# Visits of step pairs, of one output group around an attention product, or of two quarter output steps, with sums moved

## The chip, the cores and the metric

The kernel runs on one core of a Trainium2 chip. Its engines are TensorE (PE, the matmuls; PEld is its loading of weights), VectorE (DVE), ScalarE (ACT), GpSimd (POOL) and SyncE (SP, which issues transfers). SBUF is the on-chip memory that all engines read; PSUM is the small accumulator memory that PE writes, here 8 banks of 128 x 512 f32. The metric is the device time of one execution in microseconds (us).

## The reference

Attention of 8 batches, 12 heads, 448 positions and head dimension 64; its output, with the heads laid side by side, is the input of a gated feed-forward layer.

```python
scores = np.matmul(q, k.transpose(0, 1, 3, 2)) / np.sqrt(64)      # 8 x 12 x 448 x 448
attn = softmax(scores)                                             # over the last axis
x = np.matmul(attn, v).transpose(0, 2, 1, 3).reshape(3584, 768)
g, val = x @ w_gate, x @ w_val                                     # 768 -> 1536
out = (g * sigmoid(g) * val) @ w_out                               # 1536 -> 768, 3584 x 768 f32
```

## The kernel before

**The plan of visits.** Two heads make a pair, so there are 48 pairs, six to a batch. Two batches make a block of 896 tokens, held turned as `X[kk]` (768 features as 6 column blocks of 128 rows); there are four blocks. A loop (`for x, (chunks, todo) in enumerate(plan)`) walks some 50 visits. A visit issues up to three score chunks (a chunk is 128 keys of both heads against 448 queries, matmuls into the score tile `s`, L327 and L357, then one exponential on ACT, L347 or L365, into `E`), the product of one earlier pair with its values (`pv`, matmuls into two accumulators `acc`, L418), and feed-forward work. A visit without a product is called bare.

**Tiles in PSUM.** Score tiles come from the pool `ps_s`: three of two banks each. Single banks come from `ps_f`, which has two. `ps_s` also serves the gates, the output groups and the units below; `ps_f` serves the accumulators, the values and the plain outputs. A tile that is asked for waits until the last reader of the one it replaces has finished.

**A product.** `pv_open` takes the two accumulators, `pv_rest` multiplies the remaining 64 keys (8 matmuls), `pv_quad` the three full chunks (24 matmuls), and `pv_close` divides on DVE by the row sum (reciprocal L443, multiply L444). `turn_x` then transposes the result into `X` by a transfer on SP's queue (L485, L489). `copy_v` (L218, DVE) turns a pair's values into the form that the product reads; `load_v` and `load_keys` fetch them through POOL's queue (L177).

**A step** is one of 12 slices of 128 hidden units for 384 or 512 tokens: six gate matmuls (`gp`, L548), the tanh on ACT (`sg`, L573), six value matmuls (L548), and on DVE `(sg + 1) * gp` (L596) and the close, which writes `hts` (L601). `run_fv` runs one step, `run_pair` two at once with both gates ahead of the values. `run_single` runs one alone and sets `split`: the value product is then done in two halves of the tokens, the first into the second bank of the gate's score tile. A step with `late` leaves the last column block's matmuls to the end.

**An output group** (`out_group`) multiplies 256 tokens by 384 output columns as a 2 x 2 block with seven products instead of eight. Its inputs are sums: `h_sums` (L531 to L534, on `hts`) and `out_sums` (L523 to L526, on the output weights), all on DVE and all with both inputs in SBUF. Its first half is three products of six matmuls into the banks `a`, `c` and `b` of one score tile (L664). Then `p1` is kept from `a` (on ACT at L705, or with `own` on DVE at L703), `p15` from `c` (L706), and `c` is corrected from `b` (L708), for the second half adds to `c`:

```python
product(a, hh(0, x), bb(0, 0), True)
product(c, hh(0, y), tt(0))
...
apart(product(b, hs(0), tt(1), True), keep1, keep15)
nc.vector.scalar_tensor_tensor(c, p15[:], HS, b, ALU.mult, ALU.add)
yield
product(b, hs(1), tt(2))
```

The second half is products into `b`, `a`, `c` and `b`, with `part` (L712) and the last row (L718) on DVE and the first row on ACT (L683), into `osb`, which is stored.

**What sets the order.** Every engine runs its own instructions in the order in which they are emitted, so the order is that of the code. Up to visit 18 a budget (`run_budget`) deals out steps and outputs; from `base` = 19 the table `VISITS` does, one entry for each visit: the block that begins, the number of steps, of output groups, of quarter output steps (`plain_out`, 12 matmuls of 128 x 192 at L635), and of sums taken from the list `sums`:

```python
begins, nf, ng, no, ns = VISITS[x - base]
...
add_sum(ns)
if ng == 1:
    run_group(nf, gate_first=bare)
```

Here `run_group` puts a step into a group; in most visits of the table the product comes first, then a group with one step inside it, or a single step.

**After the visits**, from about 321 us, come the half block (512 tokens of `X[3]`) and then the last block of 448-wide units. In these parts `Unit` computes a gate or value product as a 2 x 2 block with seven products: P1 to P7 (PE, L778), a zero product Z (L815), A1 and A2 (ACT, L820, L824), two corrections D1 and D2 (DVE, L827, L831) that later products add to, and outputs (`out`, L843 on ACT, L845 on DVE). P1 reads the block's tokens as they are; the others need four token sums (`token_sums`, L973 to L976) and four weight sums for each unit (`weight_sums`, L741 to L744 on POOL, both inputs in SBUF). The two parts' order is worked out by `order_of`, a planner with a cost for each item; POOL's weight sums `W_5` to `W_11`, the first group's h sums `H0` to `H3` and a plain output `O` are items of it. Ahead of it stand P1 and P5 of units 0 and 1 and then the last pair's product. Behind the half block's units come its four output groups (`run_groups(groups5)`, L664), which take one sum from `sums` after each half, then the last units and the last output groups.

**Where sums lie.** `wsum_space` and `token_space` cut buffers that are free by then into the places of these sums. The half block's four token sums are emitted one to a visit in visits 47 to 50, weight sums of units 0 to 3 in visit 46 and of unit 4 after the loop. The last units' token sums (128 x 1344 each, into a buffer of the pool that holds `X`) wait in `sums` behind the second group pair's h sums and run on DVE during the half block's groups.

## Time and profile before

| | |
|---|---|
| Median of 3 runs (lowest, highest) | 449.44 us (449.36, 449.75) |
| Profiled execution | 449.9 us, of which the span is 448.1 |
| Granted TensorE clock | 1.00 |
| PE busy | 425.7 us (95%), 4594 matmuls |
| DVE, ACT, POOL busy | 268.2, 246.8, 226.3 us |
| Transfers | 50.01 MB, 112 GB/s mean |

The trace gives the following starts, in us from the start of the span:

| Place | Start |
|---|---|
| visit 13 (budget) | 91.6 |
| visit 19 (first of the table) | 125.6 |
| visit 35 | 224.3 |
| visit 46 | 289.5 |
| visit 50 | 310.2 |
| half block's units | 321.5 |
| half block's output groups | 355.7 |
| last units | 370.6 |
| end of the last output groups | 444 |

How to read the lines. In the busy table each engine has its busy time, its share of the span and its instructions (the number after x). The slices cut the span into 40 equal parts; a digit is the busy share in tenths, and 9 is 90% or more. A timeline line gives the start, the busy time, the engine, the line of the code, the operation, what it writes and from what, the tile's size, its type and a count when several instructions are drawn together; in square brackets stands how long the engine had been idle just before, with the engine, tile and line that ended the wait. An idle engine that is not the bottleneck costs nothing.

### The profile page before, as it was taken

How to read it: one execution, taken by the hardware profiler on the slowest of the kernel's cores; microseconds unless marked ns; L12 is line 12 of the kernel's file. 1: busy time of each engine (PE TensorE's matmuls, PEld its weight loads, DVE VectorE, ACT ScalarE, POOL GpSimd, SP SyncE). 2: the span in 40 equal slices, each digit the busy share in tenths (PEclk: the TensorE clock that was granted, in tenths of full speed). 3: DMA queues.
4: the chain of work that ended last, by engine and by line, in shares of the span. 5: the costliest groups of instructions: out<-in, count | busy, mean ns of one | idle time of the engine just before them, and what ended most of it. 6: DMA issues, size and time to landing. Idle time of an engine off the chain costs nothing.

```text
span 448.1 us, 11507 instructions
## 1 busy us (share of the span) xinstructions
PE 425.7 (95%) x4594; PEld 285.9 (64%) x4594; DVE 268.2 (60%) x643; ACT 246.8 (55%) x393; POOL 226.3 (51%) x349
## 2 busy tenths in 40 slices
PE   8999999999999999998999799998999899999996
PEld 3666565554647767565655576765888795555695
DVE  4666562865667655664544755556567665575663
ACT  6976677555555665745565555557365325545321
POOL 8755724999885647377357838601797000000000
PEclk9999999999999999999999999999999999999999
DMA  9999999999999999899899976313300022000124
GB/s 138 185 199 201 198 170 162 135 199 187 155 141 120 137 119 135 141 128 144 138 101 121 168 99 133 65 23 92 88 24 1 13 79 70 1 0 0 37 72 142
DMA packets 108742, 50.01 MB, mean 112 GB/s; under 512 B 60896, under 2 KB 105568, under 8 KB 108688
## 3 DMA queue, kind: packets, MB, share of 16 engines
q0 software_dynamic: 46912, 24.75, 48.3%
q1 hardware_dynamic: 61632, 24.34, 31.1%
q8 instruction: 36, 0.59, 0.5%
q14 instruction: 18, 0.15, 0.2%
q10 hardware_dynamic: 144, 0.17, 0.1%
HBM read 49.55 MB, written 11.01 MB: 135 GB/s over the span
## 4 chain that ended last, share of the span: by engine, by line
PE 77%; DVE 9%; ACT 7%; DMA 3%; issue 2%; POOL 1%; SPq 0%; DVEq 0%; POOLq 0%; ACTq 0%
PE og L664 16%; PE gp L548 14%; PE vp L548 10%; PE un L778 9%; PE ub L778 7%; PE acc L418 7%; ACT E L347 4%; PE s L327 3%; DVE hts L601 2%; PE s L357 2%; PE op L635 2%; PE acc L383 2%; DVE t L596 2%; ACT sg L573 2%; DMA qkT<-qk 1%
## 5 line engine op out<-in xcount | busy, mean ns | idle before, releaser
L347 ACT ACTIVATE E<-s 128x896 f16<-128x896 f32 x126 | 106.8, 917 | 43.2 <-PE s L327 26.9
L548 PE MATMUL gp<-X,wg 128*128 128x384 f16 (+1 forms) x360 | 74.7, 347 | 0.0
L237 POOL COPY qk<-qkraw 128x512 f16<-128x512 f16 x72 | 43.8, 648 | 58.5 <-DMA qkT<-qk 56.1
L548 PE MATMUL vp<-X,wv 128*128 128x384 f16 (+3 forms) x360 | 67.8, 326 | 0.2
L548 PEld LDWEIGHTS <-wv 128*128 128x128 f16 x444 | 42.1, 98 | 35.0 <-issue 9.4
L596 DVE SCALAR_TENSOR_TENSOR t<-sg,gp 128x384 f32<-128x384 f32 (+1 forms) x60 | 36.3, 607 | 46.4 <-ACT sg L573 35.4
L418 PE MATMUL acc<-vo,E 128*128 128x65 f16 (+1 forms) x1152 | 45.6, 193 | 6.2 <-DVE hts L601 5.4
L418 PEld LDWEIGHTS <-E 128*128 128x128 f16 (+1 forms) x1152 | 37.3, 96 | 21.3 <-issue 16.9
L625 POOL DMA_DIRECT2D out_dram<-osb x2 | 1.1, 554 | 98.3 <-DVE osb L718 98.3
L177 POOL DMA_DIRECT2D vraw<-in_v_dram x72 | 43.7, 626 | 10.5 <-DMA wo<-in_moe_w_out_dram 8.0
L573 ACT ACTIVATE sg<-gp 128x384 f32<-128x384 f32 (+1 forms) x60 | 32.0, 536 | 30.8 <-PE gp L548 30.3
L548 PEld LDWEIGHTS <-wg 128*128 128x128 f16 x360 | 32.5, 98 | 25.3 <-issue 1.9
L177 POOL DMA_DIRECT2D qkraw<-in_k_dram x70 | 42.3, 617 | 6.9 <-DMA wo<-in_moe_w_out_dram 5.3
L664 PEld LDWEIGHTS <-hts 128*128 128x128 f16 x528 | 44.1, 98 | 1.7 <-issue 1.3
L365 ACT ACTIVATE E<-s 112x896 f16<-112x896 f32 x48 | 40.4, 924 | 8.5 <-PE s L357 8.3
L601 DVE SCALAR_TENSOR_TENSOR hts<-t,vp 128x384 f16<-128x384 f32 (+3 forms) x60 | 33.2, 553 | 5.7 <-PE vp L548 2.2
L683 ACT ACTIVATE osb<-og 128x384 f32<-128x384 f32 x22 | 10.8, 491 | 40.6 <-PE og L664 36.8
L200 POOL DMA_DIRECT2D qkraw<-in_q_dram x44 | 29.8, 678 | 5.2 <-DMA vraw<-in_v_dram 1.2
L444 DVE TENSOR_TENSOR xt<-acc,R 128x256 f16<-128x256 f32 x72 | 30.6, 425 | 3.0 <-DVE R L443 0.3
L443 DVE RECIPROCAL R<-acc 128x4 f32<-128x4 f32 x72 | 12.8, 177 | 31.4 <-PE acc L418 31.4
L327 PE MATMUL s<-qkT 64*128 64x448 f16 x216 | 31.5, 353 | 0.0
L664 PE MATMUL og<-wo,hts 128*128 128x192 f16 x264 | 29.0, 246 | 0.0
(176 smaller groups left out, 725.4 us busy)
## 6 DMA issues: line engine op xcount, KB each, us to landing
vraw<-in_v_dram POOLq DMA_DIRECT2D x72, 64.0 KB, 4.7
qkraw<-in_q_dram POOLq DMA_DIRECT2D x41, 112.0 KB, 4.3
qkraw<-in_k_dram POOLq DMA_DIRECT2D x68, 64.0 KB, 4.5
wg<-in_moe_w_gate_dram POOLq DMA_DIRECT2D x8, 288.0 KB, 9.5
wv<-in_moe_w_val_dram POOLq DMA_DIRECT2D x8, 288.0 KB, 10.7
wo<-in_moe_w_out_dram POOLq DMA_DIRECT2D x2, 1152.0 KB, 19.9
out_dram<-osb SPq DMA_DIRECT2D x7, 288.0 KB, 3.5
out_dram<-osb SPq DMA_DIRECT2D x6, 336.0 KB, 3.1
```

Of the source, the lines that this page charges most:

```text
L177: eng.dma_start(dst[ts(s, 64)], rows)
L237: nc.gpsimd.tensor_copy(dst.rearrange("p c h d -> p h c d"), src)
L327: nc.tensor.matmul(s[:, hx, 0:S], lhsT=t[ts(hx, 64), ts(c + low(pr, hx), 128)], rhs=t[ts(hx, 64), ds(NC * 128, S)], start=True, stop=True,)
L347: nc.scalar.activation(e[:, 0 : 2 * S].rearrange("p (h q) -> p h q", h=2), s[:, :, 0:S], AF.Exp, scale=sm_scale)
L365: nc.scalar.activation(e[:, :, 0:S], s[0:P, :, 0:S], AF.Exp, scale=sm_scale)
L418: nc.tensor.matmul(acc[:, ts(j, D + 1)], lhsT=e[rows, ds(hx * S + j * 128, 128)], rhs=Vts[pr % NV][rows, hx, col, 0 : D + 1], start=first, ...
L548: nc.tensor.matmul(dst[:, 0:w], lhsT=wslice(kind, self.fb, cb), rhs=X[kk][:, cb, ds(c0 + lo, w)], start=(cb == 0), stop=(cb == NCB - 1),)
L573: nc.scalar.activation(self.sg[:, 0:n], gp[:, 0:n], AF.Tanh, scale=0.5)
L596: nc.vector.scalar_tensor_tensor(self.t1[:, 0:n], self.sg[:, 0:n], 1.0, self.gp[:, 0:n], ALU.add, ALU.mult)
L601: nc.vector.scalar_tensor_tensor(self.hts[:, self.fb, ds(lo, w)], self.t1[:, ds(lo, w)], 0.5 * HS, vp[:, 0:w], ALU.mult, ALU.mult)
L664: nc.tensor.matmul(dst, lhsT=lhs(n), rhs=rhs(n), start=first and n == 0, stop=n == NH - 1, skip_group_check=True)
L778: mm = nc.tensor.matmul(dst, lhsT=lhs[:, n], rhs=rhs[:, n], start=first and n == 0, stop=n == NK - 1, skip_group_check=True,)
```

## The change

The change rewrites the table, and with it what lies in the visits from 19 on.

- A visit has a pair of steps, or one output group, or two quarter output steps, or nothing; before, most had one step with or without a group. One visit has three steps, and the first still begins a block. Block 2's steps get a `late` that does nothing, so that their last column block's matmuls come last. The step that the budget kept back from block 1 (`run_fv(True)`) is now one of the pair of the first visit.
- A visit with one group (`around`) now runs `run_group_with`: the group's first half stands between the product's rest and its full matmuls, and the second half behind those. The group keeps `p1` on DVE (`own`), the first accumulator is closed ahead of the second half and the second inside it (`mid`, behind `part`). `turn_x` follows the group.
- The budget keeps a step back only at the last visit before the table, not throughout block 1.
- A visit's sums come after its steps. `run_single` marks the step `alone`, which swaps the banks of its two value halves and declares the second half independent of the gate's readers.
- From visit 19 on a pair's values are copied one visit earlier, at the end of the visit.
- The half block's token sums are emitted in visits 50 and 51, two in each, and lie partly in `Eall`. Weight sums of units 0 to 5 are emitted in visit 46; W_6 to W_11 are left to the planner.
- P1 and P5 of units 0 and 1 are left to the planner, behind the last pair's product. That product's accumulators are the two banks of one score tile (`pv_open(p0, True)`).
- The last units' four token sums move from DVE, in `sums`, to POOL, and are emitted ahead of the half block's groups.

```diff
@@ -423,8 +423,12 @@
-    def pv_open(pr):
-        accs[pr] = [ps_f.tile([128, 512], FP32, tag="f", name="acc") for _ in range(2)]
+    def pv_open(pr, one=False):
+        if one:
+            acc = ps_s.tile([128, 2, 512], FP32, tag="s", name="acc")
+            accs[pr] = [acc[:, hx] for hx in range(2)]
+        else:
+            accs[pr] = [ps_f.tile([128, 512], FP32, tag="f", name="acc") for _ in range(2)]
...
@@ -448,10 +452,13 @@
-    def pv_quad(pr):
+    def pv_pieces(pr):
...
+    def pv_quad(pr):
+        pv_pieces(pr)
...
@@ -538,13 +545,13 @@
             self.t1 = None
-            self.split = False
+            self.split = self.alone = False
...
-            for cb in cbs:
+            return [
...
@@ -580,8 +589,10 @@
                 w = self.at[2] // 2
-                dst = ps_f.tile([128, 512], FP32, tag="f", name="vp") if half else self.spare
-                self.group("v", dst, range(NCB), (half * w, w))
+                dst = self.spare if self.alone == half else ps_f.tile([128, 512], FP32, tag="f", name="vp")
+                for mm in self.group("v", dst, range(NCB), (half * w, w)):
+                    for reader in self.readers if self.alone and half else []:
+                        tc.declare_no_dep(mm.ins, reader.ins, reason="another bank")
...
@@ -593,8 +604,10 @@
                 self.t1 = fp.tile([128, 512], FP32, tag="t1", name="t1")
-                nc.vector.scalar_tensor_tensor(
-                    self.t1[:, 0:n], self.sg[:, 0:n], 1.0, self.gp[:, 0:n], ALU.add, ALU.mult
+                self.readers.append(
+                    nc.vector.scalar_tensor_tensor(
+                        self.t1[:, 0:n], self.sg[:, 0:n], 1.0, self.gp[:, 0:n], ALU.add, ALU.mult
+                    )
...
@@ -654,7 +667,7 @@
-    def out_group(kk, c0, hts, t, qw, osb, last=False, own=False):
+    def out_group(kk, c0, hts, t, qw, osb, last=False, own=False, mid=None):
...
@@ -710,6 +723,8 @@
         part = nc.vector.scalar_tensor_tensor(d, b, 1.0 / HS, p15[:], ALU.mult, ALU.add)
+        if mid:
+            mid()
...
@@ -857,7 +872,7 @@
         hts = hview(c0, n)
-        late = (lambda: turn_x(FIRST - 1)) if i == 0 else None
+        late = (lambda: turn_x(FIRST - 1)) if i == 0 else (lambda: None) if i == 2 else None
...
@@ -920,12 +935,12 @@
-            def begin(qw, own=False):
+            def begin(qw, own=False, mid=None):
                 if not qw:
                     osb.extend(new_osb() for _ in range(2))
-                return out_group(kk, c0, hts, t, qw, osb, last, own)
-            return [(lambda own=False, qw=qw: begin(qw, own), h_sums(hts, t) if not qw else []) for qw in range(2)]
+                return out_group(kk, c0, hts, t, qw, osb, last, own, mid)
+            return [(lambda own=False, mid=None, qw=qw: begin(qw, own, mid), h_sums(hts, t) if not qw else []) for qw in range(2)]
...
@@ -957,27 +972,28 @@
         VISITS = [
-            (2, 1, 0, 0, 1), (0, 2, 0, 0, 1), (0, 1, 1, 0, 0), (0, 1, 1, 0, 0), (0, 1, 0, 0, 0),
-            (0, 1, 1, 0, 0), (0, 1, 0, 0, 0), (0, 1, 1, 0, 0), (0, 2, 0, 0, 0), (0, 1, 0, 0, 0),
-            (3, 2, 0, 0, 2), (0, 1, 1, 0, 0), (0, 1, 0, 0, 0), (0, 1, 0, 1, 0), (0, 1, 1, 0, 0),
-            (0, 1, 0, 1, 0), (0, 1, 0, 1, 0), (0, 2, 0, 0, 0), (0, 1, 0, 1, 0), (0, 1, 0, 0, 0),
-            (4, 1, 0, 0, 2), (0, 1, 1, 0, 0), (0, 1, 0, 0, 0), (0, 1, 1, 0, 0), (0, 2, 0, 0, 0),
-            (0, 1, 0, 0, 0), (0, 1, 1, 0, 0), (0, 1, 0, 0, 0), (0, 1, 1, 0, 0), (0, 1, 0, 0, 0),
-            (0, 1, 0, 0, 0), (5, 0, 0, 0, 4), (0, 0, 2, 0, 0),
+            (2, 2, 0, 0, 1), (0, 2, 0, 0, 1), (0, 0, 1, 0, 0), (0, 3, 0, 0, 0), (0, 0, 1, 0, 0),
+            (0, 2, 0, 0, 0), (0, 0, 1, 0, 0), (0, 2, 0, 0, 0), (0, 0, 1, 0, 0), (0, 2, 0, 0, 0),
+            (3, 2, 0, 0, 1), (0, 2, 0, 0, 0), (0, 0, 1, 0, 0), (0, 2, 0, 0, 0), (0, 0, 1, 0, 0),
+            (0, 2, 0, 0, 0), (0, 0, 0, 2, 0), (0, 2, 0, 0, 0), (0, 2, 0, 0, 0), (0, 0, 0, 2, 0),
+            (4, 2, 0, 0, 1), (0, 2, 0, 0, 0), (0, 0, 1, 0, 0), (0, 2, 0, 0, 0), (0, 2, 0, 0, 0),
+            (0, 0, 1, 0, 0), (0, 2, 0, 0, 0), (0, 0, 1, 0, 0), (0, 2, 0, 0, 0), (0, 0, 1, 0, 0),
+            (5, 0, 0, 0, 4), (0, 0, 2, 0, 0), (0, 0, 0, 0, 0),
         ]
-        def token_sums(x, w, t):
+        def token_sums(x, w, t, eng=nc.vector):
...
-                lambda: nc.vector.tensor_sub(t[0], b12, b11),
-                lambda: nc.vector.tensor_sub(t[1], b22, t[0]),
-                lambda: nc.vector.tensor_sub(t[2], b22, b12),
-                lambda: nc.vector.tensor_sub(t[3], b21, t[1]),
+                lambda: eng.tensor_sub(t[0], b12, b11),
+                lambda: eng.tensor_sub(t[1], b22, t[0]),
+                lambda: eng.tensor_sub(t[2], b22, b12),
+                lambda: eng.tensor_sub(t[3], b21, t[1]),
...
-            return [flat[:, ts(j, NK * w)].rearrange("p (c q) -> p c q", c=NK) for j in range(4)]
+            n = min(4, flat.shape[1] // (NK * w))
+            return [flat[:, ts(j, NK * w)].rearrange("p (c q) -> p c q", c=NK) for j in range(n)]
...
@@ -1024,11 +1040,11 @@
             step = fvq.pop(0)
-            step.split = not gate_small[0]
+            step.split = step.alone = not gate_small[0]
             step.gate()
-            add_sum()
             step.value(0)
             step.finish()
+            add_sum()
...
@@ -1068,6 +1084,15 @@
             add_sum()
+        def run_group_with(p0):
+            gen = groups.pop(0)[0](True, lambda: pv_close(p0, 1))
+            next(gen)
+            add_sum()
+            pv_pieces(p0)
+            pv_close(p0, 0)
+            next(gen)
+            turn_x(p0)
...
@@ -1171,8 +1196,8 @@
         vfree = vraw[:].rearrange("p s h c d -> p (s h c d)")
-        t5 = token_space(vfree[:, 3 * 2 * NC * D :], 256)
-        tsums5 = []
+        VE = 2 * NC * D
+        t5 = token_space(Eall, 256)[0:2] + token_space(vfree, 256)[0:2]
...
@@ -1196,8 +1221,8 @@
                 add_block(0, end)
-            early = [p0 for p0 in vcopies.get(x, []) if p0 < QUAD]
-            for p0 in early:
+            early = [p0 for p0 in vcopies.get(x, []) if p0 < QUAD or x > base]
+            for p0 in early if x <= base else []:
...
@@ -1214,7 +1239,8 @@
                 add_block(adds[x], end - x)
-            for _, p0 in todo:
+            around = x > base and VISITS[x - base][1:3] == (0, 1)
+            for _, p0 in todo if not around else []:
...
@@ -1234,20 +1260,16 @@
                 extra = 2 * fvq[0].time if bare and len(chunks) == 3 and fvq and not fvq[0].at[1] else 0
-                kept_back = 2 * fvq[-1].time if fvq and adds[max(y for y in adds if y <= x)] else 0
+                kept_back = 2 * fvq[-1].time if x == base - 1 else 0
...
-                if begins == 2:
-                    run_fv(True)
                 if begins:
                     add_block(begins, 0)
-                add_sum(ns)
-                after_group = ng > 0 or nf == 1
-                if ng == 1:
-                    run_group(nf, gate_first=bare)
-                    nf = 0
+                after_group = ng > 0
+                if around:
+                    run_group_with(todo[0][1])
...
@@ -1257,7 +1279,10 @@
                     run_o()
+                if begins < 5:
+                    add_sum(ns)
                 if begins == 5:
+                    add_sum(ns)
...
@@ -1267,16 +1292,18 @@
                         wsum_space(attp.tile([128, 4 * NC * D], FP16, tag="qk16", name="wsum", bufs=3), 2)
-                    for u in range(4):
-                        weight_sums(u)
-                if x == len(VISITS) + base - 5:
-                    tsums5.extend(token_sums(X[KL - 1][:, :, 384:], 256, t5))
-                if len(VISITS) + base - 5 <= x < len(VISITS) + base - 1:
-                    tsums5[x - len(VISITS) - base + 5]()
+                    wsum_space(vfree[:, 3 * VE :], 8)
+                if x >= len(VISITS) + base - 2:
+                    tsums5 = token_sums(X[KL - 1][:, :, 384:], 256, t5)
+                    for m in range(2):
+                        tsums5[2 * (x - base - len(VISITS) + 2) + m]()
+            for p0 in vcopies.get(x + 1, []) if x >= base else []:
+                copy_v(p0)
+            if x == len(VISITS) + base - 6:
+                for u in range(6):
+                    weight_sums(u)
             while turns:
                 turn_x(turns.pop(0))
-        wsum_space(vfree, 4)
-        weight_sums(4)
...
@@ -1330,20 +1357,17 @@
         items = unit_items(units, lambda u: Unit(u, 256, x5, t5, hts5), 256)
-        for name in ("P1_0", "P1_1", "P5_0", "P5_1"):
-            items.pop(name)[3]()
         p0 = NPAIR - 1
-        pv_open(p0)
+        pv_open(p0, True)
...
-        wsum_space(Eall[:, 0 : ER * EC], 22)
+        wsum_space(Eall[:, 2 * NK * 256 : ER * EC], 18)
...
-        for u in range(5, NFB):
+        for u in range(6, NFB):
...
@@ -1368,7 +1392,9 @@
         t7 = token_space(xp.tile([128, NCB, NT], FP16, tag="X", name="T")[:].rearrange("p a b -> p (a b)"), S)
-        sums.extend(groups5[1][0][1] + token_sums(x7, S, t7))
+        sums.extend(groups5[1][0][1])
+        for fn in token_sums(x7, S, t7, nc.gpsimd):
+            fn()
```

More of the change, by code (lines that the diff above doesn't have):

```diff
@@ L554, in group @@
                 )
+                for cb in cbs
+            ]
         def gate(self):
@@ L572, in gate @@
             self.sg = fp.tile([128, 512], FP32, tag="sg", name="sg")
-            nc.scalar.activation(self.sg[:, 0:n], gp[:, 0:n], AF.Tanh, scale=0.5)
+            self.readers = [nc.scalar.activation(self.sg[:, 0:n], gp[:, 0:n], AF.Tanh, scale=0.5)]
             self.gp = gp
```

## The prediction

> **What bounds the kernel now.** I read the busy table and slices first, then TensorE's (PE's) timeline with its idle marks, then the other engines' timelines at those places.
>
> ```profile
> PE 425.7 (95%) x4594; PEld 285.9 (64%) x4594; DVE 268.2 (60%) x643; ACT 246.8 (55%) x393; POOL 226.3 (51%) x349
> PE   8999999999999999998999799998999899999996
> ```
>
> PE is the bound in every slice, so the span is PE's work, which the change leaves as it is, plus the time in which PE issues nothing. Where that is, in visit 46 and the start of 47:
>
> ```profile
> 291.12 1.14 PE L548 MATMUL gp<-X,wg 128*128 128x384 f16 x6
> 292.89 0.66 PE L548 MATMUL gp<-X,wv 128*128 128x192 f16 x6 [0.64 <-ACT sg L573]
> 294.92 0.28 PE L418 MATMUL acc<-vo,E 64*128 64x65 f16 x7 [0.24 <-DVE hts L601]
> 352.44 0.49 PE L778 MATMUL ub<-vraw,vo 128*128 128x256 f16 x3 [1.12 <-DVE un L827]
> ```
>
> A visit with a single step stalls twice: the values' first half waits for the tanh, since it writes the gate's tile, and the next visit's accumulators wait for the last `hts` write. An idle mark leaves out the drain of the last matmul: six 384-column matmuls issue in 0.98 us, so from 291.12 to 292.89 0.80 us is lost, 0.16 more than the mark says. From visit 13 (91.6 us) to 50 (313.0 us) the marks sum to 12.0 us in some 24 places; with 0.16 each, rounded down as some are part drain, 15.5 us are lost.
>
> **Visits 13 to 50 after the change.** A pair of 384-column steps already stands at 176.73 to 182.36 (5.62 us, no mark). What no visit of before does is start an output group straight behind the eight rest matmuls of the accumulators. Its score tile comes from a pool of three and is that of the visit's first score, so it waits for the first exponential:
>
> ```profile
> 138.99 0.74 PE L327 MATMUL s<-qkT 64*128 64x448 f16 x6
> 139.57 1.24 PE L418 MATMUL acc<-vo,E 64*128 64x65 f16 x32
> 140.65 0.66 PE L664 MATMUL og<-wo,hts 128*128 128x192 f16 x6
> 139.39 2.53 ACT L347 ACTIVATE E<-s 128x896 f16<-128x896 f32 x3 [1.76 <-PE s L327]
> ```
>
> The first exponential starts 0.40 after the visit and takes 0.92 (L347's mean), so the group starts at 1.37, with 0.05 to release PE (ACT's tanh to PE, 304.92 to 304.97). Then 18 group matmuls (1.48), 24 product matmuls (0.74), and the second half, which needs VectorE's (DVE's) correction of `c`. In the one group that keeps `p1` on DVE that chain is
>
> ```profile
> 148.03 0.66 PE L664 MATMUL og<-wo,hts 128*128 128x192 f16 x6
> 149.22 0.36 DVE L703 TENSOR_SCALAR p<-og 128x192 f32<-128x192 f32 x1 [1.31 <-PE og L664]
> 149.61 0.36 DVE L706 SCALAR_TENSOR_TENSOR p<-og,p 128x192 f32<-128x192 f32 x1
> 150.10 0.36 DVE L708 SCALAR_TENSOR_TENSOR og<-p,og 128x192 f32<-128x192 f32 x1
> ```
>
> 2.43 after the group's start, and PE is there at 2.22: 0.25 lost. A group visit so takes 1.37 + 2.48 + 1.98 = 5.83. The visit at 138.99 without its step takes 7.17 - 1.95 = 5.22, so each of the ten loses about 0.63: **6.3**. In visits 35, 38 and 49 an output product takes its bank behind the accumulators with no step between: by 140.48 to 141.12 (reciprocal 0.18, multiply 0.42) the first bank is free 0.52 after PE: 3 x 0.52 = **1.6**. Visit 20 waits for a close (0.69), a sum (0.55) and a second close (0.55) that stand behind visit 19's last matmul, with 0.73 of cover: **1.1**. In visit 50 the group waits for the first exponential at 1.42 while PE is there at 0.83: **0.6**. Visits behind an undivided 512-column step keep 0.15 to 0.36, as at 95.84: **1.4** for five. After: 11.0; gain 15.5 - 11.0 = **4.5 us**. For sums that fall in a bad place I allow 3 us either way. Copies of v come one visit earlier at no cost: their loads landed 25 us or more before (visits past 22). The score transposes, on SP's queue, land 14 us before use, so X's transposes moved behind the groups cost nothing.
>
> **What stands on GpSimd (POOL).** Two places put DVE instructions with both inputs in SBUF beside POOL's tensor instructions. Before:
>
> ```profile
> 339.35 0.91 POOL L744 TENSOR_TENSOR wsum<-wg,E 128x384 f16<-128x384 f16 x1
> 340.22 1.23 POOL L741 TENSOR_TENSOR vo<-wv 128x384 f16<-128x384 f16 x1
> 339.54 1.14 DVE L531 TENSOR_TENSOR hsum<-hts 128x768 f16<-128x768 f16 x1
> 354.54 0.56 DVE L532 TENSOR_TENSOR hts<-hts 128x768 f16<-128x768 f16 x1
> 365.18 0.85 DVE L973 TENSOR_TENSOR T<-X 128x1344 f16<-128x1344 f16 x1
> ```
>
> L531 began inside POOL's L744 and ended 0.42 behind it, and POOL's next took 0.32 more than L744: they took turns. At 354.54, POOL idle, the same work took 0.56.
>
> The Trainium skill, "SBUF — State Buffer", section "Who interferes with whom", says that a DVE instruction with two SBUF inputs and a GpSimd one that reads SBUF share a read interface, and that the second to issue stands still until the first has finished. The row above agrees for 0.9 us instructions; for longer ones no row here shows it. By the page the last term below is 9.0 us, without it the term's lower end of -0.6.
>
> **Start of the half-block units (321 us).** Before, four token sums lay in visits 47 to 50, with POOL idle. Now L988/L989 and the copy of v 47 stand behind the last group's `osb`, then come the closes of pair 46, then L990/L991 and pair 47's closes, while POOL's weight sums run as soon as pair 46 has been read. Counted from the last group matmul: `osb` to 0.55; L988 to 1.05; POOL 0.87; L989 to 2.4; POOL 0.9; copy to 3.55, where PE, which had s (0.2) and 32 product matmuls (0.95), could start pair 47 at 1.15: 2.45 lost. Then closes (1.15), L990 and L991 behind a POOL instruction each, four closes, first correction: 8.65, where PE (pair 47 0.85, ten short unit groups 2.2) is there at 6.65: 2.0 lost. Together 4.4; before, 1.5 (marks 0.37, 0.27 at 324 to 325 and 0.26 at 313.67, with their drains). **Cost 2.9 us**; without the turns it is 1.9 + 0.5 and pays 0.85 + 0.5 against 1.5: a gain of 0.2.
>
> **End of these units.** The units' first products are planned with the rest now, and unit 11's first correction stands ahead of its output on DVE, with two products on PE (0.66) over a chain of 0.68. The 1.12 at 352.44, with its drain 1.28, goes: **gain 1.3 us**. Late next is the product behind the second correction, 0.3 as before.
>
> **The last token sums.** Four 1344-wide subtractions (DVE, 0.85 each) go to POOL. One there takes 0.87 x 1344/384 = 3.05 us if it scales (0.1 of fixed cost would make it 2.8). They fill a buffer that the half block's X held, so they start with that block's last X product: 0.91 us after unit 11's P7 (352.44 before). On DVE there follow an output with two SBUF inputs (L845, at 0.98), and three h sums that the groups need. If turns are whole instructions: POOL to 4.0, L845, two PSUM outputs, POOL to 7.5, sum 1 to 8.1, POOL to 11.1, sum 2 to 11.65, POOL to 14.7, sum 3 to 15.25, then two corrections of `c`, 0.85. The second half of the first group starts at 16.15 instead of 6.74 (359.18 - 352.44), and its last product slips 0.6 more behind a further sum. If L845 comes first, the last product is at 16.85 instead of 7.92. Nothing covers this: the group's products are all that PE has, and the last units behind them are at 63.9 busy of 64.0. Loss 8.9 to 10.3; off it go the 0.6 that DVE's own token sums cost (0.43 at 367.88, with drain). **Cost 8.3 to 9.7; I take 9.0.** Ends: -0.6 if nothing waits; 9.7. I take the upper since 339.54 shows a wait for the rest of an instruction, to its end. The sums are done before the last units ask.
>
> **Sum:** -4.5 + 2.9 - 1.3 + 9.0 = **+6.1 us**. The profiled execution (448.1 span, 1.8 around it, 449.9) stands 0.46 above the median 449.44; from that median: **455.5 us**.
>
> **Rivals.** (1) *Long POOL instructions let DVE in* after at most 0.9 us, the longest turn in the trace: five instructions wait 0.6 each, 3.0; the first correction had 1.0 to spare (sum 3 ends at 356.29, L706 starts at 357.27): 2.0 - 0.6 = 1.4. Then -4.5 + 2.9 - 1.3 + 1.4 = -1.5: 447.9, faster. It decides when the three sums end less than about 4 us late. For: POOL could hold the port by rows. Against: 339.54. (2) *No new waits at all*, DVE slipping in ahead each time: -4.5 - 0.2 - 1.3 - 0.6 = -6.6: 442.8. Against: POOL's next is always ready, DVE's depends on its last. (3) *The visits give nothing*, h sums delaying the groups' corrections: 2.9 - 1.3 + 9.0 = +10.6: 460.0. For: 1.53 of idle at 253.63 is such a case. Against: sums are one to a visit now.
>
> **How the numbers follow.** Main case 0.62, rivals 0.17, 0.08, 0.13. The main case's own range is 452 to 459 (9.0 down to 8.3, visits by 3). Taking in the first rival, and half of the third, gives 446.5 to 460.0. A difference within 0.2% (0.9 us) can't be told from none. Slower: 0.62 + 0.13 = 0.75; the faster rivals 0.25, of which 0.03 may be the same.
>
> **What would show it.** In the profile after: no PE marks for `sg`; in ten visits a mark at `og` for the exponential (0.4) and one for L721 of 0.1; a mark at `acc` for `vo` near 316; L988 on POOL at 3 us each with h sums of 3 us beside them, and PE idle 8 us or more between the half block's units and the last ones. Wrong if POOL's subtractions are much shorter, or the h sums at 0.55 beside them; or if the idle clock gate slows PE there, which the slices of before, at full clock, can't tell.

## The result, and the profile after

The changed kernel takes 453.60 us (median; 452.76 to 456.34) against 449.50 for the kernel before (449.36 to 449.75): a ratio of 1.0101, 95% interval 1.0055 to 1.0147. It is slower by 4.1 us, where 455.5 was forecast (range 446.5 to 460.0, slower at 0.75). Its four executions spread over 3.6 us, those of the kernel before over 0.4 on this chip (on the chips of the experiments, with 7 to 19 executions, over 1.5 to 3.3), and the profiled execution (452.76, span 451.0) is the fastest of the four. Of e8, e10 and e12 below one execution each, the profiled one, ran at a lower granted clock (0.85, 0.85 and 0.94 on average), so that nothing is read from these three profiles and the times given are those of the other executions.

From the page of the changed kernel, the busy table's row and PE's slices:

```profile
PE 427.2 (95%) x4552; PEld 286.8 (64%) x4552; DVE 278.0 (62%) x641; ACT 243.1 (54%) x384; POOL 239.8 (53%) x353
PE   8999999999999999999999999999799599999996
```

PE has the same work in columns, in 42 fewer matmuls, since steps in pairs are not divided: 96 matmuls of 192 columns became 48 of 384, and 6 of 512 became 12 of 256. Its slices stand at 9 through all the visits from 13 on, where those of before fell to 8 in two places and to 7 in one; behind them come a 7 and a 5.

The windows view cuts both spans at the same points of the work: visit 13, the end of pair 46's product and of the groups around it, the plain output ahead of the half block's groups, the first of the last units, the end. Each row gives the stretch, its length and each engine's busy time, and then PE's granted clock, the transfers' share and GB/s. Before:

```profile
91.61:321.55 229.94, 217.65 (x2513) 144.65 (x2513) 137.95 (x351) 133.03 (x190) 142.47 (x228) 1.00 0.97 124
321.55:353.76 32.21, 30.15 (x289) 25.59 (x287) 21.73 (x52) 17.10 (x49) 22.35 (x25) 1.00 0.10 30
353.76:370.58 16.82, 16.30 (x182) 15.07 (x180) 11.54 (x28) 3.74 (x9) 0.00 (x0) 1.00 0.22 61
370.58:448.10 77.52, 73.23 (x532) 47.95 (x530) 43.68 (x86) 30.97 (x63) 1.09 (x2) 1.00 0.16 47
```

And after:

```profile
90.88:316.25 225.37, 217.31 (x2471) 144.00 (x2470) 137.09 (x347) 128.81 (x180) 145.58 (x231) 1.00 0.98 127
316.25:349.64 33.39, 30.01 (x293) 25.65 (x290) 25.45 (x59) 17.85 (x50) 22.16 (x24) 1.00 0.11 30
349.64:373.32 23.68, 18.62 (x183) 16.79 (x181) 18.24 (x25) 3.58 (x9) 11.06 (x4) 0.86 0.15 42
373.32:451.00 77.68, 73.22 (x532) 47.95 (x530) 42.89 (x85) 31.09 (x63) 1.09 (x2) 1.00 0.15 47
```

The visits gain 229.94 - 225.37 = 4.57. The half block's units lose 1.18, its groups lose 6.86, the last units and groups 0.16. Ahead of visit 13 another 0.73 is gained (0.54 of it a wait for a transfer in visit 12), to which the change does nothing. The sum, -4.57 + 1.18 + 6.86 + 0.16 - 0.73, is the +2.9 of the two spans. The four subtractions that POOL has in the third stretch are all that is new there.

PE's timeline at those places:

```profile
162.11 0.41 PE L418 MATMUL acc<-vo,E 64*128 64x65 f16 x8
162.91 0.66 PE L677 MATMUL og<-wo,hts 128*128 128x192 f16 x6 [0.38 <-ACT E L347]
...
318.24 1.13 PE L418 MATMUL acc<-vo,E 64*128 64x65 f16 x32 [1.84 <-DVE vo L218]
...
349.31 0.49 PE L793 MATMUL ub<-vraw,wv 128*128 128x256 f16 x3 [0.19 <-DVE kept L846]
...
355.26 1.14 PE L677 MATMUL og<-E,hts 128*128 128x192 f16 x6 [3.02 <-DVE hts L539]
358.26 1.14 PE L677 MATMUL og<-E,hsum 128*128 128x192 f16 x6 [1.85 <-DVE hsum L540]
359.19 1.17 PE L677 MATMUL og<-wo,hts 128*128 128x192 f16 x6
```

A group visit waits for the first exponential. The last pair's product waits for its copied values, and the first groups wait for h sums. From 358.26 on, the products of six 192-column matmuls begin 0.93 to 0.96 apart, where 0.50 is usual: PE's granted clock is half from 355.2 to 362.1. On POOL and on DVE stands what they wait for:

```profile
349.20 2.73 POOL L988 TENSOR_TENSOR T<-X 128x1344 f16<-128x1344 f16 x1 [10.83 <-PE un L793]
352.01 2.78 POOL L989 TENSOR_TENSOR T<-X,T 128x1344 f16<-128x1344 f16 x1
354.75 3.03 POOL L990 TENSOR_TENSOR T<-X 128x1344 f16<-128x1344 f16 x1
357.75 3.04 POOL L991 TENSOR_TENSOR T<-X,T 128x1344 f16<-128x1344 f16 x1
```

```profile
349.36 2.85 DVE L860 SCALAR_TENSOR_TENSOR hts<-silu,kept 128x256 f16<-128x256 f32 x1
352.14 0.41 DVE L860 SCALAR_TENSOR_TENSOR hts<-silu,un 128x256 f16<-128x256 f32 x1
...
352.91 2.30 DVE L539 TENSOR_TENSOR hts<-hts 128x768 f16<-128x768 f16 x1
355.24 2.96 DVE L540 TENSOR_TENSOR hsum<-hts 128x768 f16<-128x768 f16 x1
358.24 2.97 DVE L541 TENSOR_TENSOR hsum<-hts,hsum 128x768 f16<-128x768 f16 x1
...
361.57 0.36 DVE L721 SCALAR_TENSOR_TENSOR og<-p,og 128x192 f32<-128x192 f32 x1
```

Each of the four DVE instructions with both inputs in SBUF ends 0.3 to 0.4 behind the end of a POOL subtraction and holds DVE for 2.3 to 3.0 us instead of 0.4 to 0.6. The output with an input in PSUM (352.14, `un`) takes its usual 0.41 while POOL is busy.

### The profile page after: what moved, and what is told of

Its sections match the earlier page's. It is cut to its first block, busy times and chain, and to the rows that moved or that the text cites. A ratio compares the mean times of both kernels' runs of the same rounds, so it can differ in the third digit from the quotient of the medians.

```text
span 451.0 us, 11438 instructions
## 1 busy us (share of the span) xinstructions
PE 427.2 (95%) x4552; PEld 286.8 (64%) x4552; DVE 278.0 (62%) x641; ACT 243.1 (54%) x384; POOL 239.8 (53%) x353
## 4 chain that ended last, share of the span: by engine, by line
PE 70%; DMA 13%; DVE 7%; POOL 4%; ACT 3%; issue 3%; DVEq 0%; POOLq 0%
PE og L677 18%; PE gp L555 13%; PE vp L555 10%; PE un L793 9%; PE ub L793 7%; PE acc L418 6%; DMA wv<-in_moe_w_val_dram 4%; DMA qkraw<-in_k_dram 3%; PE s L327 3%; ACT E L347 3%; DMA vraw<-in_v_dram 3%; DMA wg<-in_moe_w_gate_dram 2%; POOL qkraw L200 2%; PE op L648 2%; PE op L999 1%
## 5 line engine op out<-in xcount | busy, mean ns | idle before, releaser
L237 POOL COPY qk<-qkraw 128x512 f16<-128x512 f16 x72 | 45.4, 671 | 56.8 <-DMA qkT<-qk 56.0
L555 PE MATMUL gp<-X,wg 128*128 128x384 f16 (+1 forms) x360 | 73.1, 347 | 0.0
L555 PE MATMUL vp<-X,wv 128*128 128x384 f16 (+2 forms) x360 | 69.9, 335 | 0.2
L555 PEld LDWEIGHTS <-wv 128*128 128x128 f16 x402 | 39.3, 98 | 28.8 <-issue 0.6
L677 PEld LDWEIGHTS <-hts 128*128 128x128 f16 x528 | 45.7, 99 | 9.1 <-issue 4.9
L418 PE MATMUL acc<-vo,E 128*128 128x65 f16 (+1 forms) x1152 | 44.3, 192 | 3.8 <-DVE vo L218 1.8
L614 DVE SCALAR_TENSOR_TENSOR hts<-t,vp 128x384 f16<-128x384 f32 (+2 forms) x60 | 34.5, 574 | 6.4 <-PE vp L555 4.0
L327 PE MATMUL s<-qkT 64*128 64x448 f16 x216 | 29.4, 353 | 0.0
L677 PEld LDWEIGHTS <-hsum 128*128 128x128 f16 x300 | 26.2, 100 | 3.6 <-DVE hsum L540 2.2
```

The costliest lines, as they stand in the source:

```text
L237: nc.gpsimd.tensor_copy(dst.rearrange("p c h d -> p h c d"), src)
L327: nc.tensor.matmul(s[:, hx, 0:S], lhsT=t[ts(hx, 64), ts(c + low(pr, hx), 128)], rhs=t[ts(hx, 64), ds(NC * 128, S)], start=True, stop=True,)
L418: nc.tensor.matmul(acc[:, ts(j, D + 1)], lhsT=e[rows, ds(hx * S + j * 128, 128)], rhs=Vts[pr % NV][rows, hx, col, 0 : D + 1], start=first, ...
L555: nc.tensor.matmul(dst[:, 0:w], lhsT=wslice(kind, self.fb, cb), rhs=X[kk][:, cb, ds(c0 + lo, w)], start=(cb == 0), stop=(cb == NCB - 1),)
L614: nc.vector.scalar_tensor_tensor(self.hts[:, self.fb, ds(lo, w)], self.t1[:, ds(lo, w)], 0.5 * HS, vp[:, 0:w], ALU.mult, ALU.mult)
L677: nc.tensor.matmul(dst, lhsT=lhs(n), rhs=rhs(n), start=first and n == 0, stop=n == NH - 1, skip_group_check=True)
```

## The experiments

The theory: DVE's two-SBUF-input instructions and POOL's tensor instructions take turns by whole instructions, and the long subtractions so set the groups' h sums; the visits gain; the starts of the half block's units lose to the same turns. The rivals: PE's slower clock; the sums costing as much wherever they are; the waits of the visits moving on. Times are medians with the lowest and highest, and each ratio is to the kernel before on the same chip, whose medians were 449.21 to 449.75.

### e1 and e2: the last units' token sums

e1, the changed kernel with the sums on DVE again:

```diff
-        sums.extend(groups5[1][0][1])
-        for fn in token_sums(x7, S, t7, nc.gpsimd):
-            fn()
+        sums.extend(groups5[1][0][1] + token_sums(x7, S, t7))
```

> The changed kernel with the last units' four token sums back on DVE, among the half block's groups, as before. Theory (a DVE instruction with both inputs in SBUF and a POOL one take turns by whole instructions, and the groups' h sums so come late): the stretch from the plain output (349.64 in the changed kernel) to the last units, 23.7 us, falls to the 16.8 of before; 446.0 us, granted clock 1.00 again, and the runs lie within half a microsecond of each other instead of 3.6. Rival (the lost time is the slower clock there, 0.96 instead of 0.50 for six matmuls over three microseconds): about 1.4 us are gained, 452. Rival (the sums cost as much on DVE): 453.

e2, the sums on POOL in quarters:

```diff
-        for fn in token_sums(x7, S, t7, nc.gpsimd):
-            fn()
+        b11, b12, b21, b22 = (x7[:, ts(h, NK), ts(bb, S)] for h in range(2) for bb in range(2))
+        for n in range(4):
+            cut = ts(n, S // 4)
+            nc.gpsimd.tensor_sub(t7[0][:, :, cut], b12[:, :, cut], b11[:, :, cut])
+            nc.gpsimd.tensor_sub(t7[1][:, :, cut], b22[:, :, cut], t7[0][:, :, cut])
+            nc.gpsimd.tensor_sub(t7[2][:, :, cut], b22[:, :, cut], b12[:, :, cut])
+            nc.gpsimd.tensor_sub(t7[3][:, :, cut], b21[:, :, cut], t7[1][:, :, cut])
```

> The changed kernel with the last units' token sums on POOL as there, but each cut into four quarters of its columns, 16 instructions of 128x336, all four sums of a quarter in a row. Theory (turns by whole instructions): a piece takes some 0.7 us, so each h sum ends 1.2 to 1.3 after the one ahead of it instead of 3.0; the three sums end some 3 us late instead of 5, PE loses about 2 us where it lost 6.8, and the run is about 448. Rival (POOL holds DVE back by its share of time, whatever the length of one instruction): the sums are as late as before, 453. Rival (POOL's pieces have so much fixed cost that they end much later): the last units wait for T, over 453.

Measured: e1 447.34 (446.43 to 448.95), ratio 0.9955 (0.9937 to 0.9972); e2 446.92 (446.30 to 447.89), ratio 0.9945 (0.9925 to 0.9964). The stretch from the plain output to the last units takes 16.78 in e1 (351.16 to 367.94) and 16.83 in e2 (350.66 to 367.49), instead of 23.68. So this one placement costs 6.9 us. e2 settles which property does it: there POOL does the same subtractions, in the same place and beside the same DVE instructions, in 15.2 us instead of 11.6. From DVE's timeline of e2:

```profile
350.38 0.94 DVE L860 SCALAR_TENSOR_TENSOR hts<-silu,kept 128x256 f16<-128x256 f32 x1
...
352.02 1.18 DVE L539 TENSOR_TENSOR hts<-hts 128x768 f16<-128x768 f16 x1
353.23 1.06 DVE L540 TENSOR_TENSOR hsum<-hts 128x768 f16<-128x768 f16 x1
354.33 1.06 DVE L541 TENSOR_TENSOR hsum<-hts,hsum 128x768 f16<-128x768 f16 x1
```

The sums follow each other by 1.1 to 1.2 instead of 2.3 to 3.0. POOL holds DVE back by the length of the instruction that it is in, not by its share of the time. Of the 2 us that I still expected to lose in e2 nothing was lost: a mark of 0.43 for the second sum, made good by the 0.39 for `part` that DVE's own token sums cost e1. One more miss: e1 spreads over 2.5 us, not half a microsecond. By itself that says little, for the kernel before spreads over 3.3 on the same chip; but e1's trace has half clock behind the wait at the start of the half block's units, and e6 shows a second such place.

### e3 and e4: the half block's sums, and the visits alone

e3 is e1 with the half block's token sums one to a visit again (and the weight sums and buffers that go with it); e4 is e3 with the units' first products ahead of the last product again:

```diff
-        t5 = token_space(Eall, 256)[0:2] + token_space(vfree, 256)[0:2]
+        t5 = token_space(vfree[:, 3 * VE :], 256)
...
-                if x >= len(VISITS) + base - 2:
-                    tsums5 = token_sums(X[KL - 1][:, :, 384:], 256, t5)
-                    for m in range(2):
-                        tsums5[2 * (x - base - len(VISITS) + 2) + m]()
+                if len(VISITS) + base - 5 <= x < len(VISITS) + base - 1:
+                    tsums5[x - len(VISITS) - base + 5]()
...
-                for u in range(6):
+                for u in range(4):
                     weight_sums(u)
...
+        wsum_space(vfree, 4)
+        weight_sums(4)
...
-        for u in range(6, NFB):
+        for u in range(5, NFB):
```

> The kernel of e1 with the half block's sums where they were before the change as well: its four token sums on DVE one to a visit in visits 47 to 50, in the values' buffer, and weight sums of units 0 to 3 in visit 46 and of unit 4 after the visits. Theory (at the start of the half block's units the copy of the last pair's values and the token sums take turns with POOL): the marks of 1.84 for vo and 1.36 for un at 318 to 323 go, 0.3 to 0.9 is left for the closes: 2 to 2.5 us under e1, 443.5 to 444. Rival (the accumulators in a score tile or the closes set that wait): no gain, 446.

```diff
+        for name in ("P1_0", "P1_1", "P5_0", "P5_1"):
+            items.pop(name)[3]()
         p0 = NPAIR - 1
-        pv_open(p0, True)
+        pv_open(p0)
```

> The kernel of e3 with P1 and P5 of units 0 and 1 again ahead of the last product, whose accumulators are two single banks again: what is left of the change is the visits alone. Theory: against the kernel before, the visits give 4.0 us (27.7 us between matmul starts beyond their pitch in visits 13 to 50 of before, 23.6 after): 445.0 to 445.5, and the wait of 1.1 us for the second to last correction of the half block's units is back, so e4 is 1 to 1.5 us above e3. Rival (the planned first products give nothing): e4 equals e3.

Measured: e3 444.28 (443.64 to 444.88), ratio 0.9880 (0.9851 to 0.9910); e4 446.39 (444.93 to 447.16), ratio 0.9923 (0.9896 to 0.9950). In e3 the marks of 1.84 and 1.36 at the units' start are gone and nothing takes their place. Its units' stretch is 31.3, where that of the changed kernel is 33.4 and that of e1, at half clock behind the first mark, 33.9; and this although a wait of 1.28 (1.12 and its drain) near the stretch's end is back in it. So 3.4 to 3.9 us stood at the units' start, for two token sums and a copy among POOL's weight sums.

e4 confirms the visits: with nothing else of the change they take 225.2 in its trace (229.9 before), and the kernel gains 3.0 by the medians (the profiled execution is the fastest of its five). On the end of the units it contradicts the prediction. The wait of 1.12 is in both, e3's trace

```profile
347.39 0.49 PE L793 MATMUL ub<-vraw,vo 128*128 128x256 f16 x3 [1.12 <-DVE un L842]
```

and e4's, so that the planned first products are not what removes it. What they do remove are the waits for the last product's close, in e4's trace:

```profile
319.54 0.28 PE L830 MATMUL ub<-X,ident 128*128 128x256 f16 x1 [0.37 <-DVE xt L448]
320.09 0.28 PE L830 MATMUL ub<-X,ident 128*128 128x256 f16 x1 [0.27 <-DVE xt L448]
```

With their drains (0.54 and 0.44) these are about the 0.9 by which e4's units' stretch, 32.2, is longer than e3's.

### e5 and e6: the clock, and the changed kernel again

e5 gives PE matmuls without use where it waits for h sums:

```diff
         product(a, hh(0, x), bb(0, 0), True)
+        if fills:
+            dummy(fills.pop(0))
         product(c, hh(0, y), tt(0))
+        if fills:
+            dummy(fills.pop(0))
...
+        fills.extend([12, 9])
         run_groups(groups5)
```

> The changed kernel with PE kept busy where it waits for the late h sums: 12 matmuls of 512 columns (some 2.6 us) behind the first group's first product and 9 (1.9 us) behind its second, into a single bank that nobody reads. Theory (the sums are the path; the slower clock at 355 to 362 us lies beside DVE's queue, since the correction of c ends at 361.93 and PE, at half speed, is there at 362.07): clock 1.00 in that stretch and 0.0 to 0.3 us gained. Rival (the slower clock is a good part of the 6.8 us): up to 1.4 us gained, and the runs scatter less.

> The changed kernel once more, beside the other three on the same chip: 4.1 us over the kernel before, 453.6. The stretch from the plain output to the last units takes 23.7 us, as the order of DVE and POOL sets it and not chance.

Measured: e5 455.39 (453.53 to 455.66), ratio 1.0124 (1.0100 to 1.0147); e6 455.55 (454.62 to 458.21), ratio 1.0146 (1.0112 to 1.0180). PE's timeline of e5 in the hole:

```profile
352.77 2.75 PE L163 MATMUL wp<-warm 128*128 128x512 f16 x12
355.96 0.67 PE L679 MATMUL og<-E,hts 128*128 128x192 f16 x6 [0.44 <-DVE hts L539]
...
358.96 0.67 PE L679 MATMUL og<-E,hsum 128*128 128x192 f16 x6 [0.39 <-DVE hsum L540]
359.47 0.66 PE L679 MATMUL og<-wo,hts 128*128 128x192 f16 x6
...
362.71 0.67 PE L679 MATMUL og<-E,hsum 128*128 128x192 f16 x6 [1.59 <-DVE og L727]
```

The matmuls run at full speed (0.5 apart), and PE then waits 1.59 for the correction: the stretch is 23.70, against 23.68 with the half clock. The half clock costs nothing there; DVE is the path. In e6, where the half clock (6.83 us in both traces) reached 1.5 us further into the matmuls that follow, the stretch is 24.06, so it costs 0 to 0.4.

e6's profiled execution (span 456.4) shows where the changed kernel scatters. Its visits took 229.3 instead of 225.4: 1.2 is in visit 13, where PE waits 0.56 and its first scores come late, since the steps' closes came late on DVE behind a sum that took 1.48 beside POOL's copies (L530, 1.00 in the other trace). 2.8 is the same thing in visit 20, first on PE and then on DVE:

```profile
135.12 1.11 PE L418 MATMUL acc<-vo,E 64*128 64x65 f16 x31 [1.83 <-DVE hts L614]
136.07 3.52 PE L555 MATMUL gp<-X,wg 128*128 128x384 f16 x12
139.38 2.43 PE L555 MATMUL vp<-X,wv 128*128 128x384 f16 x12
```

```profile
132.97 1.64 DVE L530 TENSOR_TENSOR qkraw<-wo,E 128x768 f16<-128x768 f16 x1
134.53 0.54 DVE L614 SCALAR_TENSOR_TENSOR hts<-t,vp 128x384 f16<-128x384 f32 x1
```

POOL had begun two copies (L237) at 132.96, 0.01 ahead of the sum, and the sum stood until both were done; behind it stood the close that the accumulators wait for; behind that wait PE ran at half clock (12 gate matmuls took 3.31, 1.94 in the other trace). In the first trace of the changed kernel the sum came 0.78 ahead of the copies and took 0.55, and the wait was 0.75.

### e7: the group's first wait taken away

e7 is e3 with a group visit's third score chunk behind the group's first half, so that the group's tile is not the one of the first chunk:

```diff
-        def run_group_with(p0):
+        def run_group_with(p0, held):
             gen = groups.pop(0)[0](True, lambda: pv_close(p0, 1))
             next(gen)
+            for u in held:
+                qk(*u)
             add_sum()
...
+            behind, held = len(held) > 0, ordered[2:] if around else []
             for n, (pr, c) in enumerate(ordered):
-                if n == 2 and (after_group or ordered[n] in quads):
+                if n == 1 + (not behind) and (after_group or ordered[n] in quads):
                     rests = open_products(rests)
-                qk(pr, c)
+                if (pr, c) not in held:
+                    qk(pr, c)
```

> The kernel of e3 with the third score chunk of each of the ten group visits issued behind the group's first half instead of ahead of the group, so that the group's score tile is the third and not the first chunk's again; in the visit that follows, the accumulators' rest matmuls are issued ahead of the second chunk. Theory (these groups wait 0.56 for the first exponential and 0.28 for the correction of c): the first wait goes, and six score matmuls more than cover the second; the next visit's second chunk takes the group's tile and waits some 0.3. Some 0.5 us for each of ten visits: 439 to 441, against 444.3 for e3. Rival (the wait only moves, to the later third exponential or to the next visit's tile): 444.

Measured: 441.50 (440.81 to 443.05), ratio 0.9835 (0.9811 to 0.9860); the visits take 222.4 where e3's take 226.2. The same visit as above, in e7:

```profile
161.56 0.60 PE L418 MATMUL acc<-vo,E 64*128 64x65 f16 x8
162.10 0.67 PE L677 MATMUL og<-wo,hts 128*128 128x192 f16 x6
...
163.69 0.36 PE L327 MATMUL s<-qkT 64*128 64x448 f16 x2
163.98 0.91 PE L418 MATMUL acc<-vo,E 128*128 128x65 f16 x24
164.72 0.66 PE L677 MATMUL og<-E,qkraw 128*128 128x192 f16 x6
```

The wait for the exponential and that for the correction are gone. The visit takes 5.63 instead of 5.93, 0.30 less and not 0.5, since the accumulators' rest matmuls, which come earlier now, wait 0.2 longer for the last step's close.

### e8 to e11: the other waits, and all together

e8 is e3 with one line ahead of the quarter outputs; e9 is the changed kernel with the sum of a pair of steps behind its last close; e10 is e7 with both and with a planner's cost:

```diff
+                out_small[0] = no > 0
                 for _ in range(no):
                     run_o()
...
             two.value(0)
-            if not small:
-                add_sum()
             two.finish()
+            if not small:
+                add_sum()
...
-            items[f"W_{u}"] = (POOL_, 3.65, [f"W_{u - 1}"], lambda u=u: weight_sums(u))
+            items[f"W_{u}"] = (POOL_, 3.5, [f"W_{u - 1}"], lambda u=u: weight_sums(u))
```

> The kernel of e3 with the first of the two quarter outputs in visits 35 and 38 put in a score tile instead of a single bank. Theory (the output waits 0.54 for the accumulators' close): two waits go, 1.1 us, 443.2 against 444.3. Rival (the score tile is late too, or missing in the next visit): 444.3. By the runs' scatter this one is read from the marks ahead of the outputs.

> The changed kernel with one line moved: in a pair of steps the sum on DVE comes behind the second step's close, not ahead of it. In one trace of the changed kernel visit 20's accumulators wait 0.75 for that close, in the other 1.83, because the sum ahead of it (L530, both inputs in SBUF) took 0.55 in the one and 1.64 in the other, where POOL's copy began 0.01 before it; behind the longer wait PE's clock was halved for 4 us, and the visits took 229.3 instead of 225.3. Theory (this race of DVE with POOL's copies makes the changed kernel's runs scatter): the close no longer waits for a sum, the wait in visit 20 is 0.3 to 0.4 every time, no slow clock follows it, and the runs lie between 452 and 453.5 instead of up to 458. Rival (the scatter is from the starts of the half block's units or from the chip): median and scatter stay, 455.

> The kernel of e7 (441.5) with the output of e8 in a score tile (two waits of 0.54), the sums behind the closes as in e9 (0.4 in visit 20, and 0.2 to 0.3 in each of the ten group visits, whose accumulators wait 0.31 for a close), and the planner's cost of a weight sum at 3.5 instead of 3.65 us, with which it puts the half block's last first correction ahead of an output again (the wait of 1.12 goes, as in the changed kernel): 441.5 - 1.1 - 0.4 - 2.5 - 1.0 = 436.5; between 436 and 439 if half of it moves on to other waits. Rival (PE's remaining waits take the place of those): 441.

> The kernel of e10 once more, for a profile at full clock: 438 to 440, and in the profile the marks of 0.54 ahead of the quarter outputs of visits 35 and 38 and the 1.12 near the end of the half block's units are gone, and the stretch from the visits' end to the plain output takes 30.3 instead of the 31.3 of e7. Rival (e10's gain on e7 was chance): 441.5, with those marks in other places.

Measured: e8 443.63 (443.46 to 444.05), ratio 0.9873 (0.9856 to 0.9889): 0.6 under e3, on another chip, which by itself decides nothing. e9 453.79 (452.43 to 454.35), ratio 1.0094 (1.0075 to 1.0112): its wait in visit 20 is

```profile
132.08 1.11 PE L418 MATMUL acc<-vo,E 64*128 64x65 f16 x31 [0.28 <-DVE hts L614]
133.03 2.11 PE L555 MATMUL gp<-X,wg 128*128 128x384 f16 x12
```

with the clock at full speed behind it, and its runs lie within 1.9 us, where the changed kernel's lay within 3.6 on either of two other chips; the kernel before lay within 2.1 on this chip and within 0.4 and 1.5 on those. The median is below e6's and above the first result's. So this race cost e6's trace its 2.8, but how much of the spread it makes is not shown; the one in visit 13 it leaves as it was. e10 438.70 (437.98 to 441.81), and e11, the same kernel again, 438.28 (437.15 to 439.52), ratio 0.9759 (0.9723 to 0.9796). In e11's trace the marks ahead of the quarter outputs in visits 35 and 38 are gone, the wait in visit 20 is 0.28, the wait of 1.12 at the end of the half block's units is gone and their stretch is 30.0 (31.3 in e7), and the visits take 220.2 (222.4 in e7). That is e7 less 3.6 in the span. The 0.2 to 0.3 that I expected from earlier closes in each group visit is not there: the accumulators' wait for the last close is as in e7. e11's busy row:

```profile
PE 425.2 (98%) x4552; PEld 283.1 (65%) x4552; DVE 272.4 (63%) x645; ACT 244.0 (56%) x384; POOL 226.6 (52%) x349
```

It beats both kernels: 2.4% under the kernel before.

### e12: the kernel before with only the token sums moved

```diff
-        sums.extend(groups5[1][0][1] + token_sums(x7, S, t7))
+        sums.extend(groups5[1][0][1])
+        for fn in token_sums(x7, S, t7, nc.gpsimd):
+            fn()
```

> The kernel before, with nothing changed but that the last units' four token sums are on POOL and emitted ahead of the half block's groups. Theory: the stretch from the plain output to the last units grows from 16.8 to 23.7 us, as in the changed kernel: 449.7 + 6.9 = 456.6, a little more where the slower clock lasts longer. Rival (the loss needs the changed kernel's other order on DVE, in which the last correction stands ahead of the outputs): 452 or less.

Measured: 456.23 (456.05 to 456.69), ratio 1.0152 (1.0122 to 1.0181), 7.0 us over the kernel before. The loss needs nothing else of the change.

## Why the prediction was right, and where it was not

The direction, the place of the loss and the case (whole turns between POOL and DVE) were right. Step by step:

- **Visits, -4.5.** The profiled pair shows -4.57, of which some 0.4 is a wait of visit 51 (0.26 at 313.67, with its drain), which the prediction booked elsewhere. The marks stand where it put them, with one exception: the exponential ahead of nine of the ten groups (the one of visit 23 waits 0.32 at its accumulators instead), 0.37 ahead of three output products (0.52 to 0.55 with the drain). A group visit takes 5.93, not 5.83: ten times 0.1 too little. The allowance for "sums that fall in a bad place" was needed: in e6 one such sum cost 2.8 with the clock behind it. Alone, the visits are worth 3.0 by e4's median and 4.8 by its trace.
- **Start of the half block's units, +2.9.** Measured 2.5 (the stretch's 1.18, and the 1.28 that its end gives back). The copy's wait was put at 2.45 lost and took 2.00, with its drain, and the first correction's at 2.0 and took 1.52. Two sums are slightly off: 3.55 less 1.15 is 2.40, and the three marks of before, with drains, are 1.4 and not 1.5.
- **End of these units, -1.3.** The size was right, 1.12 and its drain. The reason was not: that "the units' first products are planned with the rest now" does not do it (e3 has them and has the wait). What does is the planner's clock for the weight sums: with 3.5 us for each instead of 3.65 the wait goes (e11, whose other two differences from e7 lie in the visits): the last unit's first correction then stands ahead of an output on DVE, as in the changed kernel, and in e7 behind it. That the changed kernel got there because it leaves one weight sum fewer to the planner is likely and was not tested.
- **The last token sums, +9.0.** This term was mis-sized: 6.9 (e1). Two parts of it were wrong. One subtraction was scaled to 3.05 us and takes 2.73 where nothing delays it (1.3 over four), and each turn of DVE was let delay POOL by about 0.5, where POOL's next instruction started within 0.1 of its last and grew by at most 0.3 (0.9 over the rest). The upper end of the loss, 10.3, does not follow from its rows either: 16.15 less 6.74, and 0.6 more, is 10.0. The chain, the order of the turns and the instructions that wait were those of the prediction. Of its signs one did not come, PE idle for 8 us or more: in the stretch PE is idle for 5.1 (23.68 less 18.62), and for much of the rest it works at half clock.
- **Not in the sum:** the half clock, which was named as a thing that could make it wrong. It costs nothing to 0.4 in the hole (e5, e6), and some 0.5 at the start of the half block's units, whose stretch is 33.4 in two traces that lack the half clock there and 33.9 in the four that show it.

The closeness of 455.5 to 453.6 is in part luck: the profiled executions differ by 2.9, less than half of the 6.1, above all since the last term was 2.1 too large; but the profiled execution is the fastest of its kernel, and the medians on two chips lie 0.8 and 2.8 (e6) above it.

The first rival, by which long POOL instructions let DVE in after 0.9 us, is excluded by the 2.3 to 3.0 us of the four DVE rows. The second, no new waits, by the same. The third, that the visits give nothing, by e4.

## What to carry to other kernels

Before moving elementwise work from VectorE to an idle GpSimd, look at what VectorE does beside it: an instruction with both inputs in SBUF waited here for the end of the GpSimd instruction in progress, so that a long GpSimd instruction is worth as much delay as it is long, and cutting it into quarters removed a loss of 6.9 us here although the work took longer. Do not put a sum ahead of the close that TensorE waits for. And where a tile comes from a rotating pool, count whose reader it waits for: issuing one score chunk later gave back some 3 us.

## What was not expected of the hardware

- Waits of PE of 1.83 to 1.84 us were followed by half the clock for 3.41 us in five places of the traces (twice in e6, and at the start of the half block's units in e1, e2 and e5) and not in two (the changed kernel's first trace and e9, same place, same wait). What differs is where the wait falls. In the traces at full clock the granted clock changes only at whole multiples of 3.41 us from its last change (in e1 it is half from 320.58 to 324.00), which divides the span into stretches of that length. In the five places the wait lies inside one stretch; in the two a bound divides it (1.30 and 0.54 us in the first trace, 0.38 and 1.45 in e9). Up to the last matmul, every stretch at full clock with 1.62 us of waiting or less was followed by full clock, and every one with 1.83 or more by half. The Trainium skill, "TensorE: Matmul & The Clock Gate", section "HAM oscillation — how this bites in real kernels", gives as the rule no PE-idle gaps over some 3.4 us. Here gaps of little more than half of that were enough, when they fell inside one stretch.
- POOL and DVE alternate: in the three places where POOL had a next subtraction, DVE's waiting instruction went ahead of it, and POOL's next started within 0.1 of the end of its last and overlapped the end of DVE's by 0.2 to 0.5. The Trainium skill, "SBUF — State Buffer", section "Who interferes with whom", has the lock for the whole instruction, with which these rows, but for that overlap, and e2 agree; on who is next it says only that the first to issue goes first.
- A DVE copy with a single f16 input (L218) takes 0.28 alone and 0.99 between POOL's weight sums at 317.19 in the changed kernel: not only instructions with two inputs take part in the turns. The same section has it that copies can take the shared ports too.
